# Making the first column group of G and H weight by weight in a fused attention and gated-FFN kernel

## The chip, the cores and the metric

The kernel runs on one core of a Trainium2 chip. The metric is the device time of one launch in microseconds (us). The kernel before takes 829.86 us (median of six runs, 829.66 to 829.99).

## The reference, cut to what matters

```python
# B, N, C = 4, 6016, 256 ; d_ff = 1536
qn = q / (norm(q, axis=1) + 1e-6);  kn = k / (norm(k, axis=1) + 1e-6)
a  = softmax(kn.transpose(0, 2, 1) @ qn / tau)        # C x C per batch
x  = (v @ a).reshape(B * N, C)
out = (sigmoid(x @ w_gate) * (x @ w_val)) @ w_out
```

The kernel never makes `x`. It folds the attention matrix into the weights, once per batch: G = a @ w_gate and H = a @ w_val, each in three column groups of 512. The loop over the rows of v then uses G and H directly.

## The kernel before

Four parts matter: the transfers of the weight tiles, the routine that makes one product of G or H, the opening of batch 0, and the loop that begins after it. `e` is the exponential of the scores, in two halves (`e[0]`, `e[1]`), and `rrow` its two reciprocal row sums.

```python
    psg = pool("psg", 2, space=PSUM)      # two buffers each
    psv = pool("psv", 2, space=PSUM)
    pso = pool("pso", 2, space=PSUM)      # "ps_o"
    ...
    for fg in range(NFG):                 # w_gate0, w_val0, w_gate1, w_val1, ...
        for w, src in enumerate((moe_w_gate, moe_w_val)):
            nc.gpsimd.dma_start(out=w_sb[w][fg], in_=...)
    ...
    gh_order = [(0, w, i) for i in range(CB) for w in range(2)]
    gh_order += [(fg, w, i) for fg in range(1, NFG) for w in range(2) for i in range(CB)]

    def gh(b, n, pl=None, tag=None, act=None):
        fg, w, i = gh_order[n]
        ps = (pl or psm).tile([P, FG], FP32, tag=tag or "m", name="ps_gh")
        for j in range(CB):
            mm(ps, s["e"][i][:, j, :], w_sb[w][fg][:, j, :], start=(j == 0), stop=(j == CB - 1))
        ...
        if act if act is not None else n % 2 == 0:
            nc.scalar.activation(out=dst, in_=ps, func=ACT.Copy, scale=r)     # ScalarE
        else:
            nc.vector.tensor_scalar(out=dst, in0=ps, scalar1=r, ...)          # VectorE
    ...
    nc.scalar.copy(*late.pop())           # half of the transposed v
    gh_tiles(0)
    sums(0, 0)                            # row sums of half 0, reciprocal
    gh(0, 0, psg, "g", act=False)         # G(0)
    gh(0, 1, psv, "v", act=True)          # H(0)
    sums(0, 1, pss, "s")
    gh(0, 2, psg, "g", act=False)         # G(1)
    gh(0, 3, psv, "v", act=True)          # H(1)
    nc.scalar.preload_act_table(ACT.Sigmoid)
    gh(0, 4, pso, "o", act=False)         # first product of group 1
    ...
            for f in range(FC):
                glu(b, ci, f)             # gate and val products, Sigmoid, hT
                ...
                if (b, ci) == (0, 0) and f < len(gh_order) - 5:
                    gh(0, 5 + f, pso, "o")
```

## Time and profile before

| | before |
|---|---|
| time, median | 829.86 us |
| span of the profiled run | 828.0 us |
| TensorE busy | 807.7 us (98%) |
| VectorE, ScalarE busy | 591.7 us (71%), 391.1 us (47%) |
| unbroken TensorE stretch begins at | 42.96 us |

The span runs from the first to the last instruction. The last row is read from the views that the prediction shows: after 42.96 us TensorE hardly pauses. Names such as L88 are line numbers; PE, ACT and DVE are TensorE, ScalarE and VectorE. In the changed kernel the lines after 362 move up by one.

### The profile page before, as it was taken

Reading aid. Unit: us, or ns where it says so; the run is one execution under the profiler, and the core shown is the slowest. Engines: PE = TensorE matmul, PEld = TensorE weight load, DVE = VectorE, ACT = ScalarE, POOL = GpSimd, SP = SyncE. Lnnn points to the kernel's source line nnn. Section 1 sums busy time; section 2 is a strip of 40 time slices with the busy share of each in tenths; the row PEclk is TensorE's granted clock in tenths of the full one; section 3 lists DMA queues with packets and bytes.
Section 4 is the critical chain, followed back from the end, with each engine's and each line's share of the span. In section 5 each row is a group of like instructions: output and inputs, shape, how many; then the busy total and the mean of one; then the engine's idle time right before and its main releaser. Section 6 shows DMA issues by size and latency. Waiting matters only on the chain.

```text
span 828.0 us, 13639 instructions
## 1 busy us (share of the span) xinstructions
PE 807.7 (98%) x5134; PEld 498.5 (60%) x5134; DVE 591.7 (71%) x1027; ACT 391.1 (47%) x642; POOL 83.1 (10%) x159
## 2 busy tenths in 40 slices
PE   4799999999999999999999999999999999999998
PEld 3456666665665666665575666666566566666666
DVE  6777777787667777778767777777766666666665
ACT  4554444446644444445654444444655444444442
POOL 5532100002210100000311010000000000000000
PEclk8999999999999999999999999999999999999999
DMA  9999623226746443223875452223322323322211
GB/s 210 206 202 213 111 52 90 57 56 135 159 85 122 96 87 60 57 51 85 157 140 125 81 107 58 51 61 77 64 59 63 74 52 85 61 57 69 47 36 71
DMA packets 79026, 77.17 MB, mean 93 GB/s; under 512 B 50800, under 2 KB 55920, under 8 KB 78960
## 3 DMA queue, kind: packets, MB, share of 16 engines
q0 software_dynamic: 23920, 38.81, 28.3%
q1 hardware_dynamic: 54752, 36.91, 17.5%
q8 instruction: 40, 0.66, 0.3%
q10 hardware_dynamic: 288, 0.59, 0.2%
q14 instruction: 26, 0.21, 0.1%
HBM read 78.64 MB, written 24.64 MB: 125 GB/s over the span
## 4 chain that ended last, share of the span: by engine, by line
PE 94%; DMA 4%; DVE 1%; ACT 0%; issue 0%; POOL 0%; POOLq 0%
PE ps_o L88 30%; PE ps_val L88 29%; PE ps_gate L88 29%; PE ps_s L88 4%; DMA q_sb<-in_q_dram 3%; PE ps_gh L88 2%; DMA w_val<-in_moe_w_val_dram 1%; DVE hT L427 0%; ACT g_sb L426 0%; DVE sq L176 0%; PE ps_end L88 0%; ACT L531 0%; PE ps_n L88 0%; DVE gh_G L382 0%; ACT gh_H L380 0%
## 5 line engine op out<-in xcount | busy, mean ns | idle before, releaser
L427 DVE TENSOR_TENSOR hT<-ps_val,g_sb 128x512 bf16<-128x512 f32 (+1 forms) x576 | 390.9, 679 | 205.6 <-ACT g_sb L426 201.0
L426 ACT ACTIVATE g_sb<-ps_gate 128x512 bf16<-128x512 f32 (+1 forms) x576 | 338.3, 588 | 386.2 <-PE ps_gate L88 380.0
L88 PE MATMUL ps_val<-vT,gh_H 128*128 128x512 bf16 (+1 forms) x1152 | 337.5, 375 | 0.3
L88 PE MATMUL ps_gate<-vT,gh_G 128*128 128x512 bf16 (+1 forms) x1152 | 337.5, 375 | 0.0
L88 PE MATMUL ps_o<-w_out_sb,hT 128*128 128x256 bf16 x2244 | 324.8, 273 | 0.0
L88 PEld LDWEIGHTS <-hT 128*128 128x128 bf16 x2268 | 221.0, 98 | 124.6
L88 PEld LDWEIGHTS <-gh_H 128*128 128x128 bf16 x1152 | 112.7, 98 | 131.8 <-issue 1.3
L88 PEld LDWEIGHTS <-gh_G 128*128 128x128 bf16 x1152 | 112.4, 98 | 37.6 <-DVE gh_G L382 0.3
L106 POOL DMA_DIRECT2D v_sb<-in_v_dram x48 | 25.5, 532 | 620.0 <-DMA vT<-v_sb 475.0
L453 DVE COPY out_sb<-ps_o 128x256 f32<-128x256 f32 x187 | 77.2, 413 | 12.6 <-PE ps_o L88 12.6
L88 PE MATMUL ps_s<-k_sb,q_sb 128*128 128x256 bf16 x376 | 70.4, 288 | 15.6 <-DMA k_sb<-in_k_dram 8.7
L88 PEld LDWEIGHTS <-q_sb 128*128 128x128 bf16 x376 | 38.6, 103 | 24.6 <-issue 10.0
L215 DVE TENSOR_TENSOR acc<-acc,sq 128x1024 bf16<-128x1024 bf16 (+1 forms) x66 | 44.1, 669 | 0.0
L176 DVE TENSOR_TENSOR sq<-q_sb 128x1024 bf16<-128x1024 bf16 (+2 forms) x44 | 29.3, 667 | 0.0
L97 POOL DMA_DIRECT2D q_sb<-in_q_dram x48 | 26.4, 550 | 15.6 <-DMA q_sb<-in_q_dram 6.4
L97 POOL DMA_DIRECT2D k_sb<-in_k_dram x48 | 26.2, 545 | 16.2 <-DMA k_sb<-in_k_dram 7.3
L176 DVE TENSOR_TENSOR sq<-k_sb 128x1024 bf16<-128x1024 bf16 (+2 forms) x34 | 22.4, 658 | 0.2 <-DMA k_sb<-in_k_dram 0.2
L174 ACT ACTIVATE sq<-k_sb 128x1024 bf16<-128x1024 bf16 (+1 forms) x11 | 11.2, 1018 | 13.7 <-DMA k_sb<-in_k_dram 9.4
L88 PE MATMUL ps_gh<-w_gate,e_sb 128*128 128x512 bf16 x48 | 14.3, 379 | 0.4 <-DMA w_gate<-in_moe_w_gate_dram 0.4
L88 PE MATMUL ps_gh<-w_val,e_sb 128*128 128x512 bf16 x48 | 13.8, 379 | 0.5 <-DMA w_val<-in_moe_w_val_dram 0.4
L88 PEld LDWEIGHTS <-e_sb 128*128 128x128 bf16 x112 | 10.2, 98 | 5.9 <-issue 1.0
L380 ACT ACTIVATE gh_G<-ps_gh,rrow 128x512 bf16<-128x512 f32 x13 | 8.9, 687 | 8.1 <-PE ps_gh L88 6.4
(69 smaller groups left out, 120.3 us busy)
## 6 DMA issues: line engine op xcount, KB each, us to landing
out_dram<-out_sb SPq DMA_DIRECT2D x44, 512.0 KB, 2.9
v_sb<-in_v_dram POOLq DMA_DIRECT2D x44, 256.0 KB, 3.9
q_sb<-in_q_dram POOLq DMA_DIRECT2D x43, 256.0 KB, 7.3
k_sb<-in_k_dram POOLq DMA_DIRECT2D x43, 256.0 KB, 8.1
out_dram<-out_sb SPq DMA_DIRECT2D x3, 384.0 KB, 3.1
w_gate<-in_moe_w_gate_dram POOLq DMA_DIRECT2D x3, 256.0 KB, 7.9
w_val<-in_moe_w_val_dram POOLq DMA_DIRECT2D x3, 256.0 KB, 8.4
w_out_sb<-in_moe_w_out_dram POOLq DMA_DIRECT2D x1, 768.0 KB, 13.5
```

The source lines that it names most:

```text
L88: nc.tensor.matmul(out, lhsT=lhsT, rhs=rhs, start=start, stop=stop, **kw)
L97: nc.gpsimd.dma_start(out=tl[:, :nt, :], in_=rows(src, b)[:, t0 : t0 + nt, :])
L106: nc.gpsimd.dma_start(out=v_sb[:, :nt, :], in_=rows(v, b)[:, t0 : t0 + nt, :])
L174: nc.scalar.activation(out=sq[:, :nt, :], in_=src[:, :nt, :], func=ACT.Square)
L176: engine.tensor_tensor(out=sq[:, :nt, :], in0=src[:, :nt, :], in1=src[:, :nt, :], op=ALU.mult)
L215: nc.vector.tensor_tensor(out=acc[:, :nt, :], in0=acc[:, :nt, :], in1=st[b]["sq", w][:, :nt, :], op=ALU.add)
L380: nc.scalar.activation(out=dst, in_=ps, func=ACT.Copy, scale=r)
L426: nc.scalar.activation(out=g_sb[:, :n], in_=ps_gate[:, :n], func=ACT.Sigmoid)
L427: nc.vector.tensor_tensor(out=hts[b, ci][:, f, :n], in0=ps_val[:, :n], in1=g_sb[:, :n], op=ALU.mult)
L453: nc.vector.tensor_copy(out=out_sb[:, s, :], in_=ps)
```

## The change

The intent is to have a product ready for TensorE while w_val is still under way: both products of w_gate are made first, then both of w_val. The assignment of the evictions changes with it. The same list gives the order in batches 1 to 3.

```diff
-    gh_order = [(0, w, i) for i in range(CB) for w in range(2)]
-    gh_order += [(fg, w, i) for fg in range(1, NFG) for w in range(2) for i in range(CB)]
+    gh_order = [(fg, w, i) for fg in range(NFG) for w in range(2) for i in range(CB)]
...
     gh(0, 0, psg, "g", act=False)
-    gh(0, 1, psv, "v", act=True)
     sums(0, 1, pss, "s")
-    gh(0, 2, psg, "g", act=False)
+    gh(0, 1, psg, "g", act=True)
+    gh(0, 2, psv, "v", act=False)
     gh(0, 3, psv, "v", act=True)
```

## The prediction

> **What bounds the kernel now.** I read the page's chain of work first, then busy time by stretch, to see where a change in the opening could still count.
>
> ```profile
> PE 94%; DMA 4%; DVE 1%; ACT 0%; issue 0%; POOL 0%; POOLq 0%
> PE ps_o L88 30%; PE ps_val L88 29%; PE ps_gate L88 29%; PE ps_s L88 4%; DMA q_sb<-in_q_dram 3%; PE ps_gh L88 2%; DMA w_val<-in_moe_w_val_dram 1%; DVE hT L427 0%; ACT g_sb L426 0%; DVE sq L176 0%; PE ps_end L88 0%; ACT L531 0%; PE ps_n L88 0%; DVE gh_G L382 0%; ACT gh_H L380 0%
> ```
>
> TensorE carries 94% of the chain. The one transfer of the changed part that is on it is w_val. Busy time in two stretches (start:end, length, then busy us and instructions of each engine, granted clock, DMA share, GB/s):
>
> ```profile
> 36.30:42.96 6.66, 6.11 (x28) 2.55 (x29) 4.02 (x9) 5.08 (x8) 2.68 (x5) 1.00 1.23 204
> 42.96:820.00 777.04, 776.77 (x4909) 478.13 (x4909) 559.97 (x966) 368.07 (x615) 59.93 (x113) 1.00 0.43 87
> ```
>
> From 42.96 us to 820 us TensorE lacks 0.27 us of being busy in all 777.04 us. So the change can act in two ways only: move the moment at which this unbroken stretch begins, or alter the work inside it. The chain in order of time (start, us, what) shows what sets that moment:
>
> ```profile
> 29.64 7.71 DMA w_val<-in_moe_w_val_dram
> 37.35 0.04 issue
> 37.39 0.59 PE ps_gh L88 x2
> 37.98 0.03 PE ps_r L88 x2
> 38.01 0.90 PE ps_gh L88 x4
> 38.91 0.02 issue
> 38.93 0.69 ACT gh_H L380
> 39.62 0.02 issue
> 39.63 1.28 ACT L531
> 40.92 0.01 issue
> 40.93 0.61 ACT g_sb L426
> 41.54 0.02 issue
> 41.56 0.04 DVE hT L427
> 41.60 0.57 issue
> 42.17 0.75 DVE gh_G L382
> 42.92 0.04 issue
> 42.96 0.59 PE ps_gh L88 x2
> ```
>
> The first tile of w_val lands at 37.35 us. Its product H(0) is made, then G(1), then H(1); ScalarE evicts H(1), loads the Sigmoid table, makes the first gate; VectorE's first hT and then its eviction of the fifth extra product follow, and only that frees the ps_o buffer for which TensorE waits until 42.96 us. The instructions in order of time add the other side of the same microseconds (last bracket: idle before, releaser):
>
> ```profile
> 37.02 0.75 DVE L382 TENSOR_SCALAR gh_G<-ps_gh,rrow 128x512 bf16<-128x512 f32 x1 [0.67 <-PE ps_gh L88]
> ...
> 38.06 0.16 DVE L150 TENSOR_SCALAR rrow<-ps_r 128x1 f32<-128x1 f32 x1 [0.29 <-PE ps_r L88]
> 38.25 0.16 DVE L151 RECIPROCAL rrow<-rrow 128x1 f32<-128x1 f32 x1
> ```
>
> G(0) is evicted at 37.02 us, and VectorE has nothing to do before 38.06 us, because the row sums of the second half (ps_r, rrow) stand on TensorE behind H(0), which waits for w_val.
>
> **What the Trainium skill says.** "TensorE: Matmul & The Clock Gate", section "Step-by-step: what each phase is for": matmuls stay in program order; only weight loads are pulled ahead. That is why G(1), whose data is there, stands behind H(0); the trace agrees, since G(1) starts at 37.87 us, 0.48 us after H(0) at 37.39 us, though its weights w_gate had landed by 36.38 us. The same page, section "Architectural detail: the array is 16× 32×32, not 1× 128×128", says ScalarE and VectorE are strict FIFO, so an eviction cannot pass the one before it; no instruction of the window passes another. "ScalarE: Activation LUTs", section "What ACT_TABLE_LOAD costs", gives about 1283 ns for a table load plus a drain of about 1380 ns, and says that back-to-back ACTIVATEs overlap by about 93 ns. The trace has the load at 1.28 us and the Sigmoid 0.02 us after its end: no drain of that size stands here, and I use 1.28 us alone. The overlap agrees: the gh_H eviction of 0.69 us at 41.95 us is followed by a Sigmoid at 42.54 us, 0.59 us later.
>
> **The change, part by part.** Comparing the instruction order of the two built kernels, no instruction is added or removed; transfers are issued in the same order.
>
> Batches 1 to 3: two products exchange places in slots 2 and 3 of the last chunk of the batch before. Each is still 2 matmuls of 128x512, and the evictions alternate between the same two engines with the same shapes. Their results are first read some eight slots later. Cost 0.
>
> Batch 0, opening. TensorE's order becomes G(0), row sums of half 1, G(1), H(0), H(1), first product of group 1. ScalarE now evicts G(1) and H(1), VectorE evicts G(0) and H(0). Pairs of matmuls have a pitch of 0.43 us (38.73 less 38.30, or the rows of the chain after 43 us) and finish 0.59 us after they start.
>
> 1. G(0) still starts at 36.38 us when w_gate lands. The row sums and G(1) follow at 36.81 and about 36.9 us, and end by 37.5 us: the 0.41 us in which TensorE waited for w_val is filled with G(1).
> 2. H(0) starts at 37.39 us as before, H(1) at 37.82 us instead of 38.30 us, ending at 38.41 us. Taken alone this is 0.48 us off the chain.
> 3. But ScalarE now evicts G(1) first, and that needs the row sums of half 1, which VectorE can only make after its eviction of G(0). That eviction starts at 37.02 us and takes 0.75 us; a following instruction overlapped such a one by about 0.08 us (42.17 + 0.74 against a start at 42.83). So the addition starts at 37.69 to 37.79 us, the reciprocal 0.19 us later, and it ends 0.16 us after that: 38.04 to 38.14 us. ScalarE starts G(1) at about 38.07 to 38.17 us.
> 4. H(1) follows 0.59 us later, at 38.66 to 38.76 us, and takes 0.69 us: 39.35 to 39.45 us against 39.62 us. Thus 0.17 to 0.27 us of the 0.48 us survive.
> 5. Table load, first Sigmoid, first hT and the eviction move with it: 42.17 us becomes about 41.9 to 42.0 us.
> 6. TensorE must not be later than that. The first product of group 1 needs the second w_gate tile. The landing times of the three w_gate transfers are 7.7, 7.9 and 8.9 us; the first was issued at 28.42 us and took 7.9; the second, issued at 30.89 us, must then be the one of 7.7, hence 38.59 us (8.9 would be 39.79 us, after its matmul at 38.73 us). So that product starts at 38.63 us, only 0.10 us earlier than now. Six further pairs (gate, val, the next product, gate, val, product) and gate and val of the third slot, eight pairs after the first pair in all, lead to the product now at 42.96 us: 38.63 + 9 × 0.43 = 42.50 us. The eviction allows it at 42.96 − 0.27 = 42.69 us to 42.79 us. ScalarE and VectorE, not this transfer, keep the last word.
>
> From 42.69 us on the stretch is unbroken as before: the next w tiles are not needed sooner than they land, and TensorE showed no wait for transfers there. The sum is −0.17 to −0.27 us, I take −0.22 us, and 829.93 − 0.22 = 829.7 us.
>
> **The rivals.** First, the whole gain: the wait filled with a full pair, −0.43 to −0.48 us, 829.5 us. For it speaks that G(1) fits the 0.41 us gap nearly exactly; against it steps 3 and 6. Second, the gain is only moved: VectorE's row sums or the second w_gate tile take the place of the removed wait altogether, or ScalarE's two evictions do not overlap, and the time stays at 829.9 us. For it speaks that G(1)'s eviction must wait until 38.1 us at best; against it the existing pitch of 0.59 us. Third, the exchange of evictions in batches 1 to 3 holds a ps_s or ps_n buffer longer and breaks the full stretch: at most one eviction's length, 0.7 us in each of 3 batches, hence 832 us. Against it: both engines serve both buffers before and after, with equal durations of 0.69 and 0.74 us. Fourth, a colder clock: the TensorE page, section "What's actually happening", puts the loss of clock at an idle window of about 3.4 us; the granted clock is 1.00 in the window now, and the gaps there stay below half a microsecond, so no.
>
> **Range and chances.** The three timings of before span 0.33 us, more than the effect. Around 829.7 us I allow for the full gain (829.5), no gain (829.9), and 0.3 us of spread on both sides, a little more above for another chip: 829.1 to 830.2 us. Two per cent is 16.6 us; nothing here reaches a tenth of it. Chances: faster 0.005, within 2% 0.99, slower 0.005.
>
> **What would show it right or wrong.** In the profile after: TensorE without an idle gap before the first w_val product, and the gap instead before the second group's w_gate product at about 38.2 to 38.6 us (step 6); ScalarE's G(1) eviction released by VectorE's reciprocal at about 38.1 us (step 3); the Sigmoid table load at about 39.4 us instead of 39.63 us (step 4); the unbroken stretch starting at about 42.7 us (step 5); and the chain leading back through the row sums or G(0) on VectorE rather than through w_val. If the table load stays at 39.6 us, step 3 or 4 is wrong; if the unbroken stretch moves by 0.25 us and the time does not, the gain is lost behind 43 us, in the long stretch that I held to be unaffected. A transfer of w_val that lands at another time than 37.35 us in that run would shift everything and say nothing of the change.

## The result, and the profile after

The changed kernel took 829.39 us (median of six runs, 829.22 to 829.76). The ratio was 0.9995, with a 95% interval of 0.9983 to 1.0008. A ratio is the mean time of one kernel's fast runs over that of the other's of the same rounds, so it is not quite the ratio of the medians. A second comparison in later rounds (`after_again`, below) gave 829.69 against 829.92 us. The time is the same within 2%, inside the predicted range, and each interval includes 1.

The line of the page that shares out the chain of work, for the changed kernel:

```profile
PE ps_o L88 30%; PE ps_gate L88 29%; PE ps_val L88 29%; PE ps_s L88 4%; DMA k_sb<-in_k_dram 3%; PE ps_gh L88 2%; DMA w_gate<-in_moe_w_gate_dram 1%; DVE hT L426 0%; ACT g_sb L425 0%; PE ps_end L88 0%; DVE sq L176 0%; PE ps_n L88 0%; POOL q_sb L97 0%; PE ps_tp L396 0%; DVE end L467 0%
```

The transfer named is now w_gate instead of w_val. The chain in order of time (start, us, what), cut to the opening:

```profile
28.51 8.00 DMA w_gate<-in_moe_w_gate_dram
36.51 0.05 issue
36.55 0.60 PE ps_gh L88 x2
37.16 0.03 PE ps_r L88 x2
37.19 1.32 PE ps_gh L88 x6
...
40.45 0.45 PE ps_gate L88 x2
40.89 0.60 ACT g_sb L425
...
41.51 0.70 DVE hT L426
...
42.26 0.59 PE ps_val L88 x2
42.85 0.43 PE ps_gh L88 x2
```

Two things are new. TensorE no longer waits between w_gate and w_val. And after hT the chain goes straight to a val product and on; the VectorE eviction, gh_G, that stood between hT and the last product before, is gone from it. (The view names a gate product ahead of the Sigmoid at 40.89 us. The table load below ends at the same instant, 39.59 + 1.28 = 40.87 us, and the first gate product had ended long before; the experiment `before_table` shows that the table load held it.)

The instructions in order of time of the changed kernel, with rows that are not needed left out (last bracket: idle before and releaser):

```profile
37.20 0.75 DVE L381 TENSOR_SCALAR gh_G<-ps_gh,rrow 128x512 bf16<-128x512 f32 x1 [0.75 <-PE ps_r L88]
37.48 1.02 PE L88 MATMUL ps_gh<-w_val,e_sb 128*128 128x512 bf16 x4
37.87 0.15 DVE L150 TENSOR_SCALAR rrow<-ps_r 128x1 f32<-128x1 f32 x1
38.05 0.17 DVE L151 RECIPROCAL rrow<-rrow 128x1 f32<-128x1 f32 x1
38.31 0.69 ACT L379 ACTIVATE gh_G<-ps_gh,rrow 128x512 bf16<-128x512 f32 x1 [1.52 <-DVE rrow L151]
...
39.59 1.28 ACT L530 ACT_TABLE_LOAD   x1
...
41.85 0.69 ACT L379 ACTIVATE gh_H<-ps_gh,rrow 128x512 bf16<-128x512 f32 x1
42.12 0.74 DVE L381 TENSOR_SCALAR gh_G<-ps_gh,rrow 128x512 bf16<-128x512 f32 x1
42.26 0.59 PE L88 MATMUL ps_val<-vT,gh_H 128*128 128x512 bf16 x2
...
42.69 0.59 PE L88 MATMUL ps_gh<-w_val,e_sb 128*128 128x512 bf16 x2
```

ScalarE stood idle for 1.52 us until the reciprocal behind VectorE's eviction of G(0) was there, as step 3 had it. (G(1) is the second w_gate product of group 0, H(0) and H(1) the two from w_val.) The table load starts at 39.59 us, only 0.04 us earlier than before. Yet the last product shown, which I call the marked product (the second w_val product of group 1, the one at 42.96 us before), starts at 42.69 us, 0.27 us earlier, and it starts while VectorE's eviction is still running (42.12 + 0.74 = 42.86 us). Before, it waited for the end of that eviction. A wait had gone that the diff does not mention.

The built programs tell why. In the kernel before, the two ps_o buffers are handed out in strict turns: the eight products of groups 1 and 2, which I call extra, get 4, 5, 4, 5, 4, 5, 4, 5 (numbers of PSUM banks). In the changed kernel they get 4, 5, 4, 4, 5, 4, 5, 4. The marked product, the fourth, now takes the buffer that the third had just used. The third is evicted by ScalarE, which ended at 41.85 + 0.69 = 42.54 us; the buffer not taken is the one that VectorE empties; it holds the second extra product, number 5 of `gh_order`, which the prediction calls the fifth. No tile of the kernel's source asks for this. The pool chose when the program was built, and the changed order made it choose otherwise; by what rule it chooses was not looked into. The other differences in PSUM banks are small: in batches 1 to 3 G(1) and H(0) exchange banks as they exchange places (in batch 0 each keeps its own), and after the opening the ps_o buffers are used in the opposite turn.

### The profile page after: what moved, and what is told of

It is laid out like the page before. It is cut to its first block, busy times and chain, and to the rows that moved or that the text cites. A ratio compares the mean times of both kernels' runs of the same rounds, so it can differ in the third digit from the quotient of the medians.

```text
span 827.7 us, 13626 instructions
## 1 busy us (share of the span) xinstructions
PE 806.9 (97%) x5122; PEld 498.5 (60%) x5134; DVE 591.5 (71%) x1027; ACT 390.8 (47%) x642; POOL 83.1 (10%) x159
## 4 chain that ended last, share of the span: by engine, by line
PE 94%; DMA 4%; DVE 1%; issue 0%; ACT 0%; POOL 0%; POOLq 0%
PE ps_o L88 30%; PE ps_gate L88 29%; PE ps_val L88 29%; PE ps_s L88 4%; DMA k_sb<-in_k_dram 3%; PE ps_gh L88 2%; DMA w_gate<-in_moe_w_gate_dram 1%; DVE hT L426 0%; ACT g_sb L425 0%; PE ps_end L88 0%; DVE sq L176 0%; PE ps_n L88 0%; POOL q_sb L97 0%; PE ps_tp L396 0%; DVE end L467 0%
```

## The experiments

There were two theories of the gain. *Order*: it comes from filling the wait for w_val. *Buffer*: it comes from the pool's other choice. A third source, the later batches, had to be excluded too. All twelve runs below gave correct results. For each I read from the trace: g, the start of the first w_gate product; h, the start of the first w_val product; t, the start of the Sigmoid table load after the evictions; v, the start of the third val product; m, the start of the marked product.

### The two causes apart: after_rotate and before_swap

Each kernel hands out ps_o buffers by explicit names, one buffer to a name. Strict turns and the changed kernel's choice are then written down instead of left to the pool; built from the unchanged orders they reproduce both kernels' banks exactly. `after_rotate` is the changed kernel with strict turns, `before_swap` the kernel before with the other choice.

```diff
-    pso = pool("pso", 2, space=PSUM)
+    pso = pool("pso", 1, space=PSUM)
+    o_next = [0]
+    def o_tag(to=None):
+        to = o_next[0] if to is None else to
+        o_next[0] = 1 - to
+        return f"o{to}"
...                                        # every tile of pso: tag=o_tag()
+        tag = o_tag() if tag == "o" else tag or "m"                     # after_rotate
+        tag = o_tag(0 if n == 7 else None) if tag == "o" else tag or "m"  # before_swap
```

> The changed kernel, with the two ps_o buffers handed out in strict turns as in the kernel before (the pool had given the product H(1) of group 1 the buffer just used by H(0) of group 1). Measure in the trace: start of that product's first matmul, less the start of the first w_gate product (before 42.96 - 36.38 = 6.58 us, changed 42.69 - 36.55 = 6.14 us). My theory, that half of the gain is the buffer: it waits again for VectorE's eviction of the fifth product (ended 42.86 us in the changed kernel), so 42.90 - 36.55 = 6.35 us, and the time lies 0.2 us above the changed kernel's (about 829.6 us). Rival, that the order of the products is all of it: 6.14 us and 829.4 us.

> The kernel before in its own order, with only the buffer choice of the changed kernel. My theory: the product no longer waits for VectorE; it follows the val product at 42.30 us after one pitch of 0.43 us, 42.73 - 36.38 = 6.35 us, and the time is 0.2 us below before (about 829.6 us). Rival, that the order is all of it: 6.58 us, time as before 829.86 us.

`after_rotate` took 829.78 us against 829.88 us of before on the same chip (ratio 1.0000, interval 0.9987 to 1.0012), `before_swap` 829.64 us (ratio 0.9997, 0.9985 to 1.0010). The end of the wait, first `after_rotate`, then `before_swap`, in order of time, other rows left out:

```profile
41.95 0.74 DVE L389 TENSOR_SCALAR gh_G<-ps_gh,rrow 128x512 bf16<-128x512 f32 x1
42.09 0.59 PE L95 MATMUL ps_val<-vT,gh_H 128*128 128x512 bf16 x2
42.75 0.59 PE L95 MATMUL ps_gh<-w_val,e_sb 128*128 128x512 bf16 x2
```

```profile
42.00 0.74 DVE L390 TENSOR_SCALAR gh_G<-ps_gh,rrow 128x512 bf16<-128x512 f32 x1
42.14 0.59 PE L95 MATMUL ps_val<-vT,gh_H 128*128 128x512 bf16 x2
42.57 0.59 PE L95 MATMUL ps_gh<-w_val,e_sb 128*128 128x512 bf16 x2
```

With strict turns the marked product waits for the eviction's end (41.95 + 0.74 = 42.69 us) and starts 0.66 us after the val product. With the other choice it starts one plain pitch, 0.43 us, after it. The buffer is worth 0.66 − 0.43 = 0.23 us in either order, and the new order with strict turns gained nothing that the time resolves. (The time expected for `after_rotate`, about 829.6 us, was missed by 0.2 us; it had been reckoned from the changed kernel's 829.39 us of other rounds.)

The measure that I had set down, m − g, came out at 6.36 us for `after_rotate` (6.35 expected) but at 6.08 us for `before_swap` (6.35 expected). The miss has its reason in the next run.

### The same kernels again: before_again and after_again

> The kernel before, for a second trace: how far the landing of the first w tiles and the marked distance of 6.58 us vary from run to run. Expected 6.5 to 6.65 us and a ratio of 1.0000; if the distance moves by more than 0.15 us between runs, one trace cannot tell the parts apart.

> The changed kernel once more, for a second trace and a closer time. My theory: the marked product starts 6.1 to 6.2 us after the first w_gate product, and the time is 0.4 us below before (ratio 0.9995). Rival, that the 0.47 us of the first comparison was chance: ratio 1.0000.

`before_again` took 829.84 us (ratio to before, that is to itself, 0.9999, interval 0.9987 to 1.0012), `after_again` 829.69 us on the same chip, before 829.92 us (ratio 0.9997, 0.9984 to 1.0009). In `after_again` m − g was 6.13 us, as expected; its time, 0.23 us below before, lies between the expected 0.4 us and the rival's nothing. In `before_again` it was 6.23 us, against 6.58 us in the first trace of the same kernel. By my own condition one trace's m − g cannot tell the parts apart. The chain in order of time of `before_again` says what moved:

```profile
29.89 7.22 DMA w_val<-in_moe_w_val_dram
37.11 0.04 issue
37.15 0.59 PE ps_gh L88 x2
```

The same transfer that took 7.71 us in the first trace took 7.22 us here. H(0) starts 0.66 us after G(0) instead of 1.01 us. So I read each interval from its own releaser:

| trace | h − g | t − h | t − g | v − t | m − v | span − m |
|---|---|---|---|---|---|---|
| before | 1.01 | 2.24 | 3.25 | 2.67 | 0.66 | 785.0 |
| before_again | 0.66 | 2.25 | 2.91 | 2.66 | 0.66 | 785.0 |
| before_swap | 0.73 | 2.25 | 2.98 | 2.67 | 0.43 | 785.0 |
| later_only | 1.04 | 2.24 | 3.28 | 2.67 | 0.66 | 785.0 |
| after | 0.93 | 2.11 | 3.04 | 2.67 | 0.43 | 785.0 |
| after_again | 0.92 | 2.11 | 3.03 | 2.67 | 0.43 | 785.0 |
| after_rotate | 0.94 | 2.09 | 3.03 | 2.67 | 0.66 | 785.0 |

In the old order t follows H(0) by 2.24 to 2.25 us, and H(0) follows w_val; so t − g varies from 2.91 to 3.28 us with the landing. In the new order t − g is 3.03 to 3.04 us in all three traces: the chain is G(0), its eviction on VectorE, the reciprocal, and two evictions on ScalarE. The landing of w_val has dropped out of it, as long as it is not very late (`late_after`, below). The two orders break even where h − g of the old order is 3.03 − 2.245 = 0.79 us. Where w_val comes later, the new order gains; where it comes earlier, it loses. Over the four old-order rows t − g averages 3.105 us, so on these four the new order gains 0.07 us on average, from −0.12 to +0.25 us. With the buffer's 0.23 us that makes 0.30 us. The two timings gave 829.86 − 829.39 = 0.47 us and 829.92 − 829.69 = 0.23 us, on average 0.35 us. That fits, but no interval of a time proves it.

The order's 0.07 us is weaker than it looks. The traces also keep when each transfer landed, in the new order too. Over the ten traces with the transfers in their old order (`before_table`, `sums_first` and `sums_table` included) w_val lands 0.66 to 1.03 us after w_gate, on average 0.83 us, only 0.04 us above the break-even. In the profiled run of the changed kernel it was 0.68 us, so the new order lost 0.79 − 0.68 = 0.11 us there, as an estimate from the break-even. And since every trace takes 785.0 us from m to the end, within 0.1 us, the spans of the timed runs show m. Their means are 827.89 us for before, 827.96 us for `after_rotate` and 827.64 us for `before_swap` in one set of rounds, 827.89 us for before and 827.68 us for `after_again` in another, with standard errors of 0.02 to 0.09 us. The buffer alone gives −0.25 us; the order alone gives nothing that they show. So the buffer's gain is shown, and an average gain from the order is not.

### The later batches alone: later_only

```diff
+    gh_order_later = [(fg, w, i) for fg in range(NFG) for w in range(2) for i in range(CB)]
-        fg, w, i = gh_order[n]
+        fg, w, i = (gh_order if b == 0 else gh_order_later)[n]
```

> The opening as before; the new order in batches 1 to 3 only. My theory: no effect, 6.58 us in the opening and the same length of the stretch from there to the end as in the kernel before; time as before within 0.1 us. Rival, that the later batches give part of it: the stretch from the opening to the end is shorter by 0.1 us or more.

It took 830.15 us (829.74 to 830.27) against 829.88 us; ratio 1.0002, interval 0.9989 to 1.0014. The time misses my "within 0.1 us" by 0.17 us, but the trace of its slowest run (830.27 us) shows where that lies: the marked product starts at 43.21 us instead of 42.96 us, 0.22 us of this because the first w_gate tile landed later (g at 36.60 instead of 36.38 us). From the marked product to the end it takes 785.0 us, like every other trace. The later batches give nothing.

### How far the order's worth depends on the landing: four kernels

If the order pays only for a late w_val, moving that transfer should change the sign of its effect. These four kernels use strict turns, so the buffer plays no part. *late* issues the second w_gate tile ahead of the first w_val tile; *early* issues the first w_val tile ahead of the first w_gate tile. Each was made in both orders.

```diff
-    for fg in range(NFG):
-        for w, src in enumerate((moe_w_gate, moe_w_val)):
+    for w, fg in [(0, 0), (0, 1), (1, 0), (1, 1), (0, 2), (1, 2)]:   # late
+    for w, fg in [(1, 0), (0, 0), (0, 1), (1, 1), (0, 2), (1, 2)]:   # early
+        for src in ((moe_w_gate, moe_w_val)[w],):
```

> The old order of products, the ps_o buffers in strict turns, but the first w_val tile issued after the second w_gate tile, so it lands some 2.2 us after the first w_gate tile. Theory from the traces so far: in the old order the Sigmoid table load starts 2.24 us after the first w_val product (four traces: 2.24, 2.25, 2.25, 2.24), so 4.45 us after the first w_gate product, and the marked product (second product of group 1 from w_val) 3.33 us after the table load. Rival, that the order matters only through which engine evicts: the two late kernels differ by less than 0.1 us.

> The new order with the same late w_val and strict turns. Theory: G(1) is long evicted; the table load starts 2.24 - 0.48 = 1.76 us after the first w_val product (4.0 us after the first w_gate product), so the whole pair is won: 0.45 to 0.5 us less than late_before in the trace and in time. Rival: less than 0.1 us.

> The old order and strict turns, with the first w_val tile issued ahead of the first w_gate tile, so that no product waits for w_val. Theory: H(0) follows G(0) by one pitch, 0.43 us, and the table load starts 0.43 + 2.25 = 2.68 us after the first w_gate product. Rival, that the order gains whatever the landing: the early kernel in the new order is the faster.

> The new order and strict turns, with w_val first. Theory: the table load starts 3.03 us after the first w_gate product, as in three traces of this order, because ScalarE's G(1) waits for the reciprocal behind VectorE's G(0); so this order loses 0.35 us against early_before. Rival, that the order gains whatever the landing: it wins 0.1 us or more.

| kernel | h − g | t − g | m − g | time | ratio to before, interval |
|---|---|---|---|---|---|
| late_before | 2.22 | 4.47 | 7.80 | 831.36 | 1.0019, 1.0006 to 1.0032 |
| late_after | 2.17 | 3.94 | 7.26 | 830.91 | 1.0013, 1.0001 to 1.0026 |
| early_before | 0.44 | 2.69 | 6.02 | 830.37 | 1.0004, 0.9991 to 1.0016 |
| early_after | 0.92 | 3.03 | 6.35 | 830.78 | 1.0010, 0.9996 to 1.0024 |

The early pair, table load and first products, first `early_before`, then `early_after`:

```profile
37.31 0.61 PE L95 MATMUL ps_gh<-w_gate,e_sb 128*128 128x512 bf16 x2 [1.23 <-DMA w_gate<-in_moe_w_gate_dram]
...
40.00 1.28 ACT L539 ACT_TABLE_LOAD   x1
```

```profile
37.41 0.60 PE L95 MATMUL ps_gh<-w_gate,e_sb 128*128 128x512 bf16 x2 [1.43 <-DMA w_gate<-in_moe_w_gate_dram]
...
40.44 1.28 ACT L538 ACT_TABLE_LOAD   x1
```

With a late w_val the new order wins 0.53 us to the table load and 0.45 us in the medians; with an early one it loses 0.34 us and 0.41 us. The sign turns as the break-even says, on one chip in one set of rounds. The traces show it; the intervals of the times overlap within each pair. In `late_after` w_val sets the table load again, 3.94 us after g instead of 3.03 us. Both rivals (that only the evicting engine matters, that the order always gains) fall. The medians of all four lie above before's 830.00 us because either other issue order delays a tile that the opening needs: the late one H(0), to 2.2 us after G(0), the early one G(0), to 37.3 and 37.4 us instead of 36.4 to 36.6 us.

### What limits the new order, and a version that goes further: sums_first, before_table, sums_table

`sums_first` makes both row sums ahead of G(0). `before_table` is the kernel before with the Sigmoid table load moved ahead of the four evictions, where ScalarE is idle. `sums_table` is the changed kernel with both edits.

```diff
     nc.scalar.copy(*late.pop())
+    nc.scalar.preload_act_table(ACT.Sigmoid)  # before_table, sums_table
...
     sums(0, 0)
+    sums(0, 1, pss, "s")                      # sums_first, sums_table
     gh(0, 0, psg, "g", act=False)
-    sums(0, 1, pss, "s")
...
-    nc.scalar.preload_act_table(ACT.Sigmoid)  # before_table, sums_table
```

> The changed kernel with both row sums made ahead of the first product, so that the reciprocal of half 1 no longer stands behind VectorE's eviction of G(0). My theory (step 3 of the prediction): ScalarE starts G(1) when its matmul ends, about 1.1 us after the start of the first w_gate product instead of 1.76; the Sigmoid table load starts at 2.7 us after it instead of 3.04; the marked product at 5.85 to 5.90 us instead of 6.14, then bound by TensorE itself and the second w_gate tile; time 0.25 us below the changed kernel. Rival, that VectorE's place is irrelevant and the first tiles' landing sets it: 6.14 us, no change.

> The kernel before, with the Sigmoid table loaded ahead of the four evictions, while ScalarE is idle (36.7 to 38.0 us). My theory, that the table load after the last eviction is what turns the late H(1) into a late start: the first gate follows its matmul, the marked product is then bound by TensorE alone, 38.73 + 9 x 0.43 = 42.61 us, 6.23 us after the first w_gate product instead of 6.58; time 0.35 us below before. Rival, that w_val's landing sets it: 6.58 us.

> The changed kernel with both row sums first and the Sigmoid table loaded ahead of the evictions. My theory: bound by the second w_gate tile and TensorE: the marked product 9 x 0.43 = 3.87 us after the first product of group 1, without any stall between; 5.85 us after the first w_gate product if that tile lands 1.95 us after the first as in the changed kernel's trace; time about 0.3 us below the changed kernel, the lowest of all. Rival, that something else of the opening holds it: a stall remains between and the distance stays above 6.0 us.

`sums_first`: 829.44 us against 829.88 us (ratio 0.9996, 0.9982 to 1.0009). ScalarE starts G(1) 1.07 us after g (1.1 expected), the table load comes at 2.64 us (2.7), the marked product at 5.92 us (5.85 to 5.90), 0.51 us after the val product, 0.08 us more than the plain pitch, so a short wait is left. Its pool made the changed kernel's choice of buffers. The forecast of a time 0.25 us below the changed kernel was not tested, as that kernel was not in these rounds. The line of ScalarE shows the releaser changed from the reciprocal to the matmul itself:

```profile
37.61 0.69 ACT L379 ACTIVATE gh_G<-ps_gh,rrow 128x512 bf16<-128x512 f32 x1 [0.86 <-PE ps_gh L88]
```

`before_table`: 829.61 us against 829.92 us (ratio 0.9995, 0.9981 to 1.0009). The marked product comes 42.58 − 37.35 = 5.23 us after the first w_val product, where 42.61 − 37.39 = 5.22 us was expected; in the kernel before it is 5.57 us. One moved line in the old order thus gives 0.34 us, a little more than the 0.30 us reckoned above for the whole change; in the same rounds it took 829.61 us and the changed kernel 829.69 us. (The m − g expected, 6.23 us, was 6.00 us, since w_val came early again.) The first Sigmoid now follows its gate product instead of the table load:

```profile
39.76 0.60 ACT L426 ACTIVATE g_sb<-ps_gate 128x512 bf16<-128x512 f32 x1 [0.17 <-PE ps_gate L88]
```

`sums_table`: 829.47 us against 829.92 us (ratio 0.9995, 0.9982 to 1.0007); in the same rounds the changed kernel had 829.69 us (829.50 to 829.74) and this one 829.32 to 829.61 us, so its median is 0.45 us below before and 0.22 us below the changed kernel: the lowest of these rounds, though again by too little for an interval. From the first product of group 1 to the marked one it takes 42.58 − 38.70 = 3.88 us, the nine plain pitches expected (3.87); nothing stalls there any more. The rest is the second w_gate tile, for which TensorE idles 0.25 us before that first product; it landed 0.2 us later after g than I had assumed: m − g was 6.06 us, not 5.85. So the rival was right that it stayed above 6.0 us, but the stall lies in front, in a transfer. Its pool went back to strict turns, and with the early table load that no longer matters.

## Why the prediction was right or wrong

The time lay in the predicted range and on the predicted side. Its parts fared differently.

- **The bound** (the change acts only on the start of the unbroken stretch): right. From the marked product to the end all seven traces of the table took 785.0 us, and the four late and early kernels agree to 0.1 us (829.3 − 44.30 = 785.0 for `late_before`).
- **Batches 1 to 3 cost nothing**: right, shown by `later_only`.
- **Steps 1 and 2** (TensorE filled, H(1) earlier): right. The four w_val matmuls follow w_gate's without a wait.
- **Steps 3 and 4** (G(1) waits for the reciprocal behind G(0)'s eviction, two ScalarE evictions with a pitch of 0.59 us): right in mechanism and size. A table load at 39.35 to 39.45 us less 36.38 us is 2.97 to 3.07 us; 3.03 to 3.04 us was measured, with a pitch of 38.89 − 38.31 = 0.58 us. `sums_first` confirms the cause.
- **The gain of step 4** ("0.17 to 0.27 us of the 0.48 us survive") failed in size. It took the landing of one trace, w_val 1.01 us behind w_gate, for a property of the kernel. Old-order traces with the transfers in their old order put H(0) 0.66 to 1.04 us after G(0), `before_table` (0.77) included. The term averages 0.07 us over four traces instead of 0.22, and can be negative. Over all ten traces that show the landing it is about 0.04 us. In the profiled run of the changed kernel itself the table load came 0.04 us earlier. My last sentence had set such a landing aside as something that "would shift everything"; it does not, since at these landings only the old order depends on it.
- **Step 5** ("Table load, first Sigmoid, first hT and the eviction move with it", so that the eviction "allows it" at 42.69 to 42.79 us, step 6) failed: I kept the release of the marked product by VectorE's eviction. The pool had moved that product to the other buffer. The term that I had at zero measured 0.23 us in the three traces of the table with that choice, and 0 in the four with strict turns. It can be seen without running anything, from the buffers in the two built programs; I had compared the order of the instructions and not their buffers.
- **Step 6**, that the second w_gate tile holds TensorE a little: right. The tile landed at 38.47 us and its product began at 38.51 us (38.63 predicted); a plain pitch would have allowed 37.48 + 2 × 0.43 = 38.34 us. As said there, this is not the last word until the table load is out of the way.
- **Two of my signs misled**, because the first w_gate tile landed 0.17 us later in this run (g at 36.55 instead of 36.38 us). A table load at 39.6 us was to prove step 3 or 4 wrong; it came at 39.59 us, and yet both steps held, counted from g. The unbroken stretch was to start at about 42.7 us, and 42.69 us was measured: that is luck. Counted from g it is 6.14 us, where steps 5 and 6 gave 6.31 to 6.41 us; the later tile hid most of the buffer's 0.23 us. `after_rotate`, which has the wait that I had assumed, gave 6.36 us.

Thus −0.22 us was predicted from the order. About −0.3 us came, 0.23 us of it from the buffer and the rest, which is not shown to differ from nothing, from the order. That the second timing gave −0.23 us, nearly the number predicted, is luck too. Of the rivals, the "whole gain" had nearly the right time (829.5 us) with a wrong mechanism, which shows how little one time says here. The moved wait held in part: in `early_after` the reciprocal behind G(0) takes more than the whole gain. The later batches and the colder clock did not occur; the granted clock was 1.00 from 36.30 to 42.96 us in both kernels.

## What to carry to other kernels

When a change alters the order in which tiles are taken from a pool, compare which buffers they get in the two builds, not only the order of the instructions: a tile may come to wait on another engine, as here. A wait for a transfer that is seen in one trace is a sample; look at two or three traces before counting on its length, and prefer intervals between an instruction and its own releaser to intervals from a distant start. Filling a wait helps only as far as the filler's own followers (here a reciprocal behind an eviction) do not take its place.

## What the Trainium skill lacked or had wrong

- "ScalarE: Activation LUTs", section "What ACT_TABLE_LOAD costs": the load itself agrees (1.28 us), but of the drain of about 1380 ns nothing is seen here; the load follows the last eviction by 0.01 us (38.93 + 0.69 against 39.63) and the Sigmoid follows the load by 0.02 us.
- No page that I read says how far the landing of one transfer varies from run to run: from issue to landing the same 256 KB tile took 7.71 and 7.22 us in two traces of one kernel, enough to turn the sign of what the order gives (h − g of 1.01 and 0.66 us around the break-even of 0.79 us).
- No page that I read says that a pool's buffers may be handed out other than in turns, and that a reorder elsewhere can change it: here 0.23 us.
